# Gate and up products of the last feature pairs as seven block products, and shorter column steps

## The chip, the cores and the metric

The kernel runs on one core of a Trainium2 chip. The metric is the device time of one execution in microseconds (us): the median of the runs. The core has a matrix engine (TensorE, PE in the profile; its weight loads are PEld), VectorE (DVE), ScalarE (ACT), GpSimd (POOL) and SyncE (SP). Each runs its own instruction stream in the order in which the program emitted it, and they are kept together by semaphores. SP's and POOL's queues issue the transfers here.

## The reference

Two branches work on 2048 tokens of 576 channels and are mixed by a gate that depends on the token:

```
g = sigmoid((A_x * gate_w).sum(-1))
a = irfft2(rfft2(A_x) * (w_r + 1j * w_i))           # over tokens and channels
b = (gelu_tanh(B_x @ w_gate) * (B_x @ w_up)) @ w_down   # 576 -> 4608 -> 576
out = g * a + (1 - g) * b
```

Branch a is called the spectral branch here, branch b the dense branch. The kernel uses one input, x, for both.

## The kernel before

**The dense branch** keeps PE busy. Tokens are split in two halves `p` of 1024, each in two blocks `tb` of 512; the 4608 hidden features in 36 tiles of 128, taken two at a time, so there are 18 feature pairs for each half and 36 in all. A number is split in two parts of reduced precision, hi and lo, and a product is hi·hi + lo·hi + hi·lo. The 576 channels are four tiles of 128 and a tail of 64; the tail stands twice in one tile, so that two matmuls do its three products. So gate, or up, of one feature tile for one token block is a `chain` (L642) of 4 x 3 + 2 = 14 matmuls of 128x512 into one PSUM bank (`pgu`, two buffers). `hidden` (L675) runs the gate chain, GELU on ACT out of PSUM, the up chain, the multiplication on DVE (L688), a copy that rounds to hi on ACT (L204 is the helper of all such copies) and the low part on DVE (L693). `down` (L718) multiplies a hidden block of two features and 128 tokens with the down weights: 2 x 6 matmuls of 128x288 (L704) into `pdn`, an ACT copy that scales by 1 - g into a staging buffer (L728), and a transfer on POOL's queue that adds it to the result in DRAM (L716). Weights are loaded into `raw` (L615, L616), and split by an ACT copy and a DVE subtraction (L623).

The main loop (L842) runs over slots, one for each pair and token block: 4 chains, and 4 `down`s of the slot before. At the end (`down_end`, L761, and `down_last`, L747) the sums are read back from DRAM, added on DVE (L754) and stored to the output. Between the halves the token operands are reloaded (`reload_x`, L833; L607).

**The spectral branch** is a Python generator, `spectral` (L528): FFTs along channels on DVE for two halves of the tokens (`forward_rows`), FFTs over 16 tiles (`dft16_tiles`), 16 column blocks (`columns`, L221) with two small matrix products each on PE (`product`, L258, into `pf`, one buffer), and the way back (`inverse_rows`, L478, for each half). Its instructions are put among those of the dense branch:

- After 1 to 9 matmuls the dense branch calls `gap()` (L564): twice in each chain (L652), once in each `down` (L730), so 12 times a slot. `gap` first runs what is due at that count (`later`, filled by `at(n, fn)`: n gaps from now), then one entry of `aux`, then the generator.
- The generator is stepped while `credit[0]` is positive. `tick` (L556) adds `RATE` times the PE time of the matmuls; each step and each DVE instruction of the dense branch takes off its own cost. `yield None` ends the gap.
- `lower` (L620) makes a weight tile's low part due three gaps on; `due` (L629) runs it at once if a matmul needs it sooner.

A column step in `columns` is `STEP` = 9 gaps long (L303): the first product (g = 0), the filter on DVE (L291, L292, L299 to L301, L337, L338), the second product (g = 5) on the previous block, rounding copies and lows (L256) ahead of each, and `corner` (L243), which moves two 64-partition pieces of a tile over SP's queue, out to `cns` and back in a later gap.

Of the kernel before, what the change touches and what calls it, by code (L numbers as in the profile page):

```python
# [24 lines left out]
KT = 5  # L25
# [3 lines left out]
UNIT = ROWS // 4  # L29
RATE = 0.9  # L30
STEP = 9
ROW_BLOCK = (0, 6, 3, 5, 8, 1, 2, 7, 4)
# [125 lines left out]
def _build(nc, tc, a):  # L158
    with ExitStack() as ctx:
# [17 lines left out]
        dn = [mk(f"dn{i}", [2, D], F32R) for i in range(4)]  # L177
        raw = [mk(f"raw{i}", [KT * 256 + D]) for i in range(2)]
        hb = [mk(f"hb{i}", [2, TB], F32R) for i in range(3)]
# [41 lines left out]
        def columns():  # L221
# [62 lines left out]
            for kb in range(18):  # L284
# [18 lines left out]
                for g in range(STEP):  # L303
                    if g == 0:
                        if on:
                            v = product(0, kb, xh, xl)
                            load_ww(kb + 1)
                            corner(kb + 2, 0, False)
                        if was:
                            copy(yh, vs)  # L310
                    elif g == 1 and on:
                        copy(zr, v[:, 1, :NK])
                        vec.tensor_tensor(two(w1), two(w1), sgn[:, None, :].to_broadcast([P, 2, NK]), ALU.mult)
                    elif g == 2:
                        if was:
                            low(yl, vs, yh)
                        if kb + 1 < 16:
                            copy(xh2, two(Z[kb + 1]))
                    elif g == 3:
                        if on:  # L320
                            filter_start()
                        corner(kb - 2, 2, True)
                    elif g == 4:
                        if on:
                            corner(kb + 2, 0, True)
                        if kb + 1 < 16:
                            low(xl2, two(Z[kb + 1]), xh2)
                    elif g == 5:
                        if was:
                            w = product(1, kb - 1, yh, yl)  # L330
                        if on:
                            swap()
                    elif g == 7:
# [5 lines left out]
                    elif g == 8:  # L339
# [4 lines left out]
                    if kb == 17 and g > 5:  # L344
                        break
                    credit[0] -= 0.6 if on else 0.0
                    yield None
# [130 lines left out]
        def inverse_rows(h):  # L478
# [6 lines left out]
            yield from stage(rows, 32, range(4), 1)  # L485
            yield from small_twiddles(rows, LEFT, 1)
            yield from stage(rows, 8, range(4), 1)
            r1, r2, r3, r4, z0, i1, i2, i3, i4 = (rows[:, 512 * i:512 * (i + 1)] for i in range(9))
# [18 lines left out]
            R = rows.rearrange("p (k t) -> p t k", t=8)  # L507
            yield None
            for t in range(8):
# [108 lines left out]
        todo = {}  # L618

        def lower(key, g, r, cost):  # L620

            def run():
                vec.tensor_tensor(g[:, 1], r, f(g[:, 0]), ALU.subtract)  # L623
                credit[0] -= cost

            todo[key] = run
            at(3, lambda: due(key))

        def due(key):  # L629
            todo.pop(key, lambda: None)()  # L630

# [65 lines left out]
        def down_mm(ps, prev, t, part):  # L697
            c = slice(t * P, (t + 1) * P)
            j, h = prev[3][part]
            due(("dn", j))  # L700
# [17 lines left out]
        def down(prev, t):  # L718

            p, i, tb, _ = prev  # L720
            u = 8 * p + 4 * tb + t
# [18 lines left out]
        def rest(i):  # L740
            return st[i][:, 0:D]

# [17 lines left out]

        def down_end(prev):  # L761
            f = ps_f2()
            ps = [pair(), pair(), (f[:, 0, 0:HD], f[:, 1, 0:HD]), (ps_gu()[:, 0:HD], ps_gu()[:, 0:HD])]
            for t in range(4):
                down_last(prev, t, ps[t], 0)
            for t in range(4):
                down_last(prev, t, ps[t], 1)

# [71 lines left out]
        lows = []  # L840
        nslot = 2 * NBLK * 2
        for n in range(nslot + 1):  # L842
            p, r = divmod(n, 2 * NBLK)
            i, tb = divmod(r, 2)
            j = 2 * (p * NBLK + i)
            last = n == nslot
            if n == 2 * NBLK - 2:
                for q in range(4):
                    load_x(q)
            if n == nslot - 2:  # L850
                while gens:
                    credit[0] = 1.0
                    gap()
                for u in range(8):
                    nc.sync.dma_start(a["y"][u], yd[u])
                load_last(0)
            if n == nslot - 1:
                load_last(1)
            if n in (2 * NBLK - 1, 2 * NBLK):
                reload_x(1 - tb)  # L860
            if last:
                lows.pop()()
                down_end(prev)
                break
            ends = n == nslot - 1
            def early():
                if lows:
                    lows.pop()()

            h0, low0 = hidden(j, tb, early)  # L870
            if ends:
                for t in range(2):
                    v = pair()
                    for part in range(2):
                        down_last(prev, t, v, part)
            elif prev is not None:
                down(prev, 0)
                down(prev, 1)
            low0()
            jn = j + 2 + tb  # L880
            more = jn < 2 * NT and n > 0
            if n == 1:
                prep_gu(2)
                prep_dn(2)
            if more:
                prep_gu(jn)
            hprev = prev

            def mid():
                if ends:  # L890
                    for t in range(2, 4):
                        v = pair()
                        for part in range(2):
                            down_last(hprev, t, v, part)
                elif hprev is not None:
                    down(hprev, 2)
# [3 lines left out]
            if more:  # L900
                prep_dn(jn)
                for q in ((4, 5) if n == 1 else (jn + 2,)):
                    if q < 2 * NT:
                        at(3, lambda q=q: load_w(q))
            lows.append(low1)
            prev = (p, i, tb, ((j, h0), (j + 1, h1)))

# [49 lines left out]
```

## Time and profile before

| | |
|---|---|
| median of 3 runs | 1421.62 us (1421.54 to 1423.27) |
| profiled execution | 1421.89 us, span from first to last instruction 1420.1 us |
| busy: PE, DVE, ACT, POOL | 1409.4, 885.8, 641.2, 264.3 us |
| column stage (first to last product) | 458.9 to 726.5 us |
| last small twiddle of the way back, second half (L126) | 1058.9 us |
| last store of the spectral branch (L521) | issued at 1135.1 us |
| granted TensorE clock, mean | 0.998 |

A row that groups instructions gives: line, engine, operation, output <- input, shapes, count | busy us, mean ns | idle us of the engine before them, and what ended it. A row of the order of time gives: start us, duration us, engine, line, operation, and in brackets an idle time before it with its releaser. A row of waits gives: engine, tile and line that waited, what it waited for, total us, times, longest. A row of windows gives: stretch, length, then busy us and (count) of PE, PEld, DVE, ACT and POOL, the granted clock, the DMA engines' busy share and GB/s. A row of one line's instructions gives: engine, operation, output <- input, count: least, median and largest ns, first and last start in us. A row of transfers gives: target <- source, queue, count, KB each, median us from issue to landing. PE's durations are modelled and overlap; its pitch is read from the starts.

### The profile page before, as it was taken

How to read it: one execution, taken by the hardware profiler on the slowest of the kernel's cores; microseconds unless marked ns; L12 is line 12 of the kernel's file. 1: busy time of each engine (PE TensorE's matmuls, PEld its weight loads, DVE VectorE, ACT ScalarE, POOL GpSimd, SP SyncE). 2: the span in 40 equal slices, each digit the busy share in tenths (PEclk: the TensorE clock that was granted, in tenths of full speed). 3: DMA queues.
4: the chain of work that ended last, by engine and by line, in shares of the span. 5: the costliest groups of instructions: out<-in, count | busy, mean ns of one | idle time of the engine just before them, and what ended most of it. 6: DMA issues, size and time to landing. Idle time of an engine off the chain costs nothing.

```text
span 1420.1 us, 19578 instructions
## 1 busy us (share of the span) xinstructions
PE 1409.4 (99%) x7686; PEld 1245.2 (88%) x7686; DVE 885.8 (62%) x1160; ACT 641.2 (45%) x956; POOL 264.3 (19%) x321
## 2 busy tenths in 40 slices
PE   9999999999999999999999999999999999999998
PEld 7888888888888889888888888888888888888887
DVE  5978758797785656655658878774878522222223
ACT  5534454444454555555645453436343533333331
POOL 0011121111112122222110211114111321111110
PEclk9999999999999999999999999999999999999999
DMA  7466666556668789899863556569656776665754
GB/s 258 147 121 118 116 163 120 105 111 120 120 112 202 178 200 197 207 227 197 212 141 121 109 100 111 112 121 186 114 96 115 143 144 120 121 112 110 163 96 123
DMA packets 90813, 201.94 MB, mean 142 GB/s; under 512 B 11104, under 2 KB 21344, under 8 KB 90336
## 3 DMA queue, kind: packets, MB, share of 16 engines
q0 software_dynamic: 44928, 90.98, 43.0%
q1 hardware_dynamic: 45792, 109.70, 24.7%
q8 instruction: 60, 0.98, 0.3%
q14 instruction: 33, 0.27, 0.1%
HBM read 101.48 MB, written 92.01 MB: 136 GB/s over the span
## 4 chain that ended last, share of the span: by engine, by line
PE 98%; DMA 1%; ACT 0%; SPq 0%; DVE 0%; issue 0%; DVEq 0%
PE pdn L704 32%; PE pgu L647 18%; PE pgu L649 18%; PE pgu L648 18%; PE pgu L654 5%; PE pgu L653 5%; PE pf L263 2%; DMA til<-xt 1%; DVE til L754 0%; ACT stg L728 0%; ACT gu L204 0%; SPq L779 0%; SPq L778 0%; PE pf L704 0%; PE pgu L704 0%
## 5 line engine op out<-in xcount | busy, mean ns | idle before, releaser
L704 PEld LDWEIGHTS pdn<-dn,hb 128*128 128x128 f32 x3432 | 471.6, 188 | 11.3 <-ACT til L204 0.2
L704 PE MATMUL pdn<-dn,hb 128*128 128x288 f32 x3432 | 479.3, 295 | 0.0
L647 PE MATMUL pgu<-xhi,gu 128*128 128x512 f32 x1144 | 447.7, 391 | 1.3 <-ACT gl L682 1.3
L649 PE MATMUL pgu<-xlo,gu 128*128 128x512 f32 x1144 | 446.5, 390 | 0.0
L648 PE MATMUL pgu<-xhi,gu 128*128 128x512 f32 x1144 | 446.3, 390 | 0.0
L716 POOL DMA_DIRECT2D yd<-stg x264 | 230.3, 873 | 1070.2 <-ACT stg L728 1031.8
L688 DVE TENSOR_TENSOR gl<-gl,pgu 128x512 f32<-128x512 f32 x144 | 98.9, 687 | 336.6 <-PE pgu L654 336.3
L204 ACT ACTIVATE hb<-gl 128x512 fp32r<-128x512 f32 x144 | 91.2, 633 | 438.9 <-DVE gl L688 438.9
L728 ACT ACTIVATE stg<-pdn,omg 128x576 f32<-128x576 f32 x272 | 201.7, 742 | 168.1 <-PE pdn L704 165.8
L649 PEld LDWEIGHTS pgu<-xlo,gu 128*128 128x128 f32 x1144 | 215.0, 188 | 46.6
L647 PEld LDWEIGHTS pgu<-xhi,gu 128*128 128x128 f32 x1144 | 215.1, 188 | 40.9 <-ACT gl L682 1.7
L648 PEld LDWEIGHTS pgu<-xhi,gu 128*128 128x128 f32 x1144 | 215.0, 188 | 39.0
L623 DVE TENSOR_TENSOR gu<-raw,gu 128x1280 fp32r<-128x1280 f32 x70 | 104.3, 1489 | 79.0 <-ACT gu L204 78.7
L685 ACT ACTIVATE gl<-pgu 128x512 f32<-128x512 f32 x143 | 85.5, 598 | 144.1 <-PE pgu L654 143.9
L693 DVE TENSOR_TENSOR hb<-gl,hb 128x512 fp32r<-128x512 f32 x144 | 99.0, 688 | 31.1 <-ACT hb L204 30.9
L653 PE MATMUL pgu<-xtl,gu 128*128 128x512 f32 x286 | 111.4, 389 | 0.0
L654 PE MATMUL pgu<-xtl,gu 128*128 128x512 f32 x286 | 111.4, 389 | 0.0
L204 ACT ACTIVATE gu<-raw 128x1280 fp32r<-128x1280 f32 (+2 forms) x77 | 92.2, 1197 | 4.9 <-DMA raw<-wgu 4.6
L653 PEld LDWEIGHTS pgu<-xtl,gu 128*128 128x128 f32 x286 | 53.7, 188 | 11.3
L654 PEld LDWEIGHTS pgu<-xtl,gu 128*128 128x128 f32 x286 | 53.7, 188 | 11.1
L623 DVE TENSOR_TENSOR dn<-raw,dn 128x576 fp32r<-128x576 f32 x72 | 54.1, 751 | 1.3 <-ACT dn L204 1.3
L92 DVE TENSOR_TENSOR rows<-rows 128x1280 f32<-128x1280 f32 x36 | 53.6, 1489 | 0.7
(116 smaller groups left out, 862.6 us busy)
## 6 DMA issues: line engine op xcount, KB each, us to landing
yd<-stg POOLq DMA_DIRECT2D x264, 288.0 KB, 5.1
raw<-wgu SPq DMA_DIRECT2D x70, 640.0 KB, 5.5
raw<-wd SPq DMA_DIRECT2D x72, 288.0 KB, 2.8
colm<-col POOLq DMA_DIRECT2D x32, 256.0 KB, 5.9
tmp<-wf SPq DMA_DIRECT2D x16, 290.0 KB, 5.4
cns<-til SPq DMA_DIRECT2D x64, 72.5 KB, 4.9
til<-cns SPq DMA_DIRECT2D x64, 72.5 KB, 4.3
misc<-wf SPq DMA_DIRECT2D x16, 290.0 KB, 5.5
```

Source lines behind the costliest of these rows:

```text
L204: act.activation(o, i, AF.Copy)
L623: vec.tensor_tensor(g[:, 1], r, f(g[:, 0]), ALU.subtract)
L647: pe.matmul(ps, w[:, 0, k, c], xhi[tb][:, k], start=k == 0, stop=False)
L648: pe.matmul(ps, w[:, 1, k, c], xhi[tb][:, k], start=False, stop=False)
L649: pe.matmul(ps, w[:, 0, k, c], xlo[tb][:, k], start=False, stop=False)
L653: pe.matmul(ps, w[:, 0, 4, c], xtl[tb], start=False, stop=False)
L654: pe.matmul(ps, w[:, 1, 4, c], xtl[tb], start=False, stop=True)
L688: vec.tensor_tensor(g, g, pu, ALU.mult)
L693: vec.tensor_tensor(h[:, 1], g, f(h[:, 0]), ALU.subtract)
L704: pe.matmul(ps[half], h[:, l, c], d[:, q, half * HD:(half + 1) * HD], start=part == 0 and n == 0, stop=part == 1 and n == 2)
L716: pl.dma_start(yd[u], o, accum_op=ALU.add)
L728: put(u, lambda o: act.activation(o.rearrange("p (c k) -> p c k", c=2), v[:, :, 0:HD], AF.Copy, scale=omg[:, u:u + 1]), i == 0)
```

## The change

**Block products.** For the second half of the tokens, gate and up of a pair are seen as a 2x2 block product: two token blocks by two halves of the channels (288 each), times two halves of the channels by two feature tiles. Seven block products with sums and differences of blocks (Strassen, in Winograd's form) give the same four results as eight. A half of the channels is two tiles of 128 and a tail of 32 that stands four times in one tile, so one matmul does the tail. One block product of one of gate and up is 2 x 3 + 1 = 7 matmuls (`seven`), a product has two of these. The seven products write to `pgu` and `pf` in turn; DVE adds each to running sums in SBUF; for each finished block GELU, multiplication, copy and low follow in later gaps.

The weights of the seven products (`prep_b`) are differences of blocks on DVE, then hi (ACT, 768 columns) and low (DVE, 512 columns on 128 and 256 on 64 partitions), two products ahead, in four slots of the old `gu` buffers. The token operands are built once by the generator `operands`, after the spectral branch has freed its memory, and `late_operands` adds one that needs the buffers of the ordinary chains.

**The switch.** `inverse_rows(1)` sets `free` after its small twiddles. The pair that then begins still loads weights as before, the next one loads the first blocks, and from there on pairs are done by `products`; with this schedule these are the last nine. `finale` takes the place of `down_end`. The second half's spectral result is now added through the staging buffers (`put`), one every four gaps.

**Spectral pace.** `RATE` is 0.95 instead of 0.9, a column step has 7 gaps instead of 9 and takes 6.4 instead of 5.4 of credit. The first product stays at g = 0; the filter moves from g = 3 to 2, ahead of the low that was at 2; the second product from g = 5 to 4; the corner's way back on the second side from four gaps after its way out to two, on the first side from four to three.

`lower` and the new preparations go through `seq`, which makes several steps due at several counts; `due` now runs all that are left.

The diff, cut to its core (new helpers `tail_of`, `late_operands`, `load_b`, `load_d` and the host's packing are left out; `load_b` and `load_d` issue the loads on SP's queue):

```
-RATE = 0.9
-STEP = 9
+RATE = 0.95
+STEP = 7
...
-                    elif g == 1 and on:
-                        copy(zr, v[:, 1, :NK])
-                        vec.tensor_tensor(two(w1), two(w1), sgn[:, None, :].to_broadcast([P, 2, NK]), ALU.mult)
+                    elif g == 1:
+                        if on:
+                            copy(zr, v[:, 1, :NK])
+                            vec.tensor_tensor(two(w1), two(w1), sgn[:, None, :].to_broadcast([P, 2, NK]), ALU.mult)
+                        if kb + 1 < 16:
+                            copy(xh2, two(Z[kb + 1]))
+                        corner(kb - 2, 2, True)
                     elif g == 2:
+                        if on:
+                            filter_start()
                         if was:
                             low(yl, vs, yh)
...
                     elif g == 3:
                         if on:
-                            filter_start()
-                        corner(kb - 2, 2, True)
...
-                    elif g == 5:
+                    elif g == 4:
                         if was:
                             w = product(1, kb - 1, yh, yl)
...
+        def seq(key, *steps):
+
+            q = todo[key] = [fn for _, fn in steps]
+            for n, _ in steps:
+                at(n, lambda: q and q.pop(0)())
+
+        def due(key):
+            q = todo.pop(key, [])
+            while q:
+                q.pop(0)()
...
+        def prep_b(i, m, lead=0):
...
+            def total():
+                for o, p, q in ((), (), ((r11, r12, r11), (tsum, r22, r11)), ((r12, r22, r12),), (),
+                                ((r21, r21, tsum),), ())[m]:
+                    vec.tensor_tensor(o, p, q, ALU.subtract)
+                    credit[0] -= 0.95
+
+            def high():
+                copy(w[:, 0:768], x)
+
+            def low():
+                vec.tensor_tensor(w[:, 768:1280], x[:, 0:512], f(w[:, 0:512]), ALU.subtract)
+                vec.tensor_tensor(w[64:128, 512:768], x[64:128, 512:768], f(w[64:128, 512:768]), ALU.subtract)
...
+            seq(("b", i, m), (lead, total), (lead + 2, high), (lead + 4, low))
+
+        def seven(ps, i, m, x, s):
+
+            due(("b", i, m))
...
+            for t in range(2):
+                c = slice(256 * t + P * s, 256 * t + P * (s + 1))
+                pe.matmul(ps, hi[:, c], xh[:, t], start=t == 0, stop=False)
+                pe.matmul(ps, lo[:, c], xh[:, t], start=False, stop=False)
+                pe.matmul(ps, hi[:, c], xl[:, t], start=False, stop=False)
+            pe.matmul(ps, w[:, 512 + P * s:512 + P * (s + 1)], xt, start=False, stop=True)
+            tick(7 * 0.2265)
+            gap()
+
+        def products(i, spare, pend, early):
...
+                seq((name, i), (1, lambda: act.activation(g, g, AF.Gelu_apprx_tanh)), (2, mult),
+                    (3, lambda: copy(h[:, 0], v)), (5, low))
...
+            for n, (name, nd) in enumerate((("a11", 2), ("a12", 2), ("s2", 1), ("s3", 1), ("s1", 1), ("a22", 1),
+                                            ("s4", 0))):
+                m = n + 2
+                prep_b(i + m // 7, m % 7, 2 if m in (7, 9) else 0)
...
+                if n % 2:
+                    y = ps_f2()
+                    ps = [y[:, s] for s in range(2)]
+                else:
+                    ps = [ps_gu() for _ in range(2)]
+                for s in range(2):
+                    seven(ps[s], i, n, name, s)
+                    due({1: ("c12", i - 1), 3: ("c21", i - 1), 4: ("c11", i), 6: ("c22", i)}.get(n))
+                    if n == 0:
+                        copy(u[s], ps[s])
+                    for o, x in (((), ((c, u),), ((u, u),), ((u3, u),), ((c, u3), (u, u)), ((u3, u3),), ((c, u),))[n]):
+                        add(o[s], x[s], ps[s])
+                    if n == 0 and s == 0:
+                        early()
+                k = {1: ("c11", c), 4: ("c22", c), 5: ("c21", u3), 6: ("c12", c)}.get(n)
+                if k:
+                    finish(*k)
+                for _ in range(nd):
+                    if pend:
+                        d, t = pend.pop(0)
+                        down(d, t)
...
+            if state or p == 1 and tb == 0 and free[0]:
+                state += tb == 0
+            if state == 3:
+                break
...
+        late_operands()
...
+        for i in range(i, NBLK):
...
+            products(i, spare, pend, early)
+        finale(pend)
```

In `finale` the four `down`s of the second token block run one after another, then those of the first block in four PSUM places, all first parts ahead of all second parts.

More of the change, by code (lines that the diff above doesn't have):

```diff
@@ L508, in inverse_rows @@
             yield None
+            if h == 1:
+                yield from operands()
+                for t in range(8):
+                    u = 8 + t
+                    put(u, lambda o: act.activation(o, R[:, t, 0:D], AF.Copy, scale=gs[:, u:u + 1]), False)
+                    for _ in range(4):
+                        yield None
+                return
             for t in range(8):
@@ L759, in pair, with tail_of @@
             return v[:, 0, 0:HD], v[:, 1, 0:HD]
[L761 to L767, printed above, removed]
+        ops = {}
+        free = [False]
+        def tail_of(o, x):
+            copy(o, x)
+            for q in (32, 96):
+                r = slice(q, q + 32)
+                vec.tensor_tensor(o[r], x[r], f(o[r]), ALU.subtract)
```

224 lines of the change are left out of this document (170 added, 54 removed).

## The prediction

> **What bounds the kernel now.** I read the page first (busy time, slices, chain), then the waits of the matrix engine, then windows and the order of time where something was odd.
>
> ```profile
> span 1420.1 us, 19578 instructions
> PE 1409.4 (99%) x7686; PEld 1245.2 (88%) x7686; DVE 885.8 (62%) x1160; ACT 641.2 (45%) x956; POOL 264.3 (19%) x321
> DVE  5978758797785656655658878774878522222223
> PE 98%; DMA 1%; ACT 0%; SPq 0%; DVE 0%; issue 0%; DVEq 0%
> PE pf L263 <- ACT gu L204: 2.9, 1, 2.9
> PE pgu L647 <- ACT gl L682: 1.3, 1, 1.3
> ```
>
> PE is the chain (98%), and its only wait after the start is one of 2.9 us. Only fewer matmuls or a shorter matmul can make this kernel faster; whatever delays PE by a microsecond makes it that much slower. VectorE (DVE) has room in the last seven slices, where the spectral branch has ended, and little before.
>
> The price of a matmul comes from the order of time, since the listed durations overlap:
>
> ```profile
> 1199.10 0.39 PE L647 MATMUL pgu<-xhi,gu 128*128 128x512 f32 x1
> ...
> 1202.27 0.39 PE L647 MATMUL pgu<-xhi,gu 128*128 128x512 f32 x1
> ...
> 1205.45 3.35 PE L704 MATMUL pdn<-dn,hb 128*128 128x288 f32 x24
> 1205.72 0.69 DVE L688 TENSOR_TENSOR gl<-gl,pgu 128x512 f32<-128x512 f32 x1 [3.60 <-PE pgu L654]
> 1206.44 0.63 ACT L204 ACTIVATE hb<-gl 128x512 fp32r<-128x512 f32 x1 [3.31 <-DVE gl L688]
> 1207.10 0.69 DVE L693 TENSOR_TENSOR hb<-gl,hb 128x512 fp32r<-128x512 f32 x1 [0.70 <-ACT hb L204]
> ...
> 1208.63 0.40 PE L647 MATMUL pgu<-xhi,gu 128*128 128x512 f32 x1
> ```
>
> From 1199.10 to 1205.45 are two chains of 14: 3.18 us a chain, 0.227 us a matmul. 24 down matmuls take 1208.63 - 1205.45 = 3.18 us, so one `down` takes 1.59 us. A pair of features has 8 chains and 8 downs: 38.2 us. DVE begins 0.27 us after the next PE work would begin (1205.72 against 1205.45).
>
> **The block products.** A pair's 8 chains (112 matmuls) become 7 products of 14 (98): one chain, 3.18 us, saved a pair, and 9 x 3.18 = **28.6 us** for nine pairs. Shapes are the same (128x512 moving), so the pitch is kept. The downs stay 8 a pair.
>
> For that, DVE and ACT work more. The nearest rows:
>
> ```profile
> L688 DVE TENSOR_TENSOR gl<-gl,pgu 128x512 f32<-128x512 f32 x144 | 98.9, 687 | 336.6 <-PE pgu L654 336.3
> L623 DVE TENSOR_TENSOR gu<-raw,gu 128x1280 fp32r<-128x1280 f32 x70 | 104.3, 1489 | 79.0 <-ACT gu L204 78.7
> L800 DVE TENSOR_TENSOR gu<-raw,gu 128x256 fp32r<-128x256 f32 x5 | 2.1, 423 | 3.8 <-ACT gu L204 3.8
> ```
>
> Per pair DVE does 14 additions out of PSUM (0.687 each, 9.6 us), 4 weight differences of 768 columns (between 0.687 and 1.489, by length 0.955: 3.8), 7 weight lows of 512 and of 256 columns (0.69 + 0.423: 7.8), 2 down lows of 576 (by length 0.755: 1.5), and for 4 hidden blocks a product and a low (0.687 + 0.69 each: 5.5): 28.2 us, against 10.0 before (2 x 1.489 + 1.5 + 5.5). A pair will take 35 to 37 us, so DVE is about 77% busy. That is what it is in the window 40 to 456 quoted below, where PE never waits. ACT gets some 19 us a pair. So the engines have the capacity, and the cost lies in the **order** of DVE's queue. I went through one pair with these durations, product by product (14 matmuls, then its downs; 2, 2, 1, 1, 1, 1, 0 of them). A product's sums must be out of PSUM before the second next product uses the same banks. They are: the fifth product's four additions end 1.5 us after it, and the seventh begins 6.4 us after it (two downs and a product). Seven being odd, the next pair's first product takes the seventh's banks at once, but half by half, and the first half's addition is out 0.6 us before (1.59 - 0.27 - 0.69). The weights are ready too, with one exception.
>
> That is the border between two pairs. The weights of the next pair's first product are prepared with a lead of 2, so their low is due at 6 gaps, and only 5 gaps come (two half products and one down, then two half products and no down). It is therefore forced by `due` when that product begins, and it stands in DVE's queue behind the last additions of the seventh product, which wait for PE. From the end of that product: 0.27 until DVE starts, 0.69 addition, 0.69 low, and 0.15 back to PE (the row pair 4.55 + 0.42 to 5.12, below) make 1.8 us; PE has one matmul to do meanwhile (0.23). **1.6 us at each of 8 borders, 12.8 us.** Bounds: 0, if the low comes earlier than I read; 2.9 (the only wait of PE this trace has) each.
>
> ```profile
> 4.55 0.42 DVE L803 CAST xhi<-til 128x512 fp32r<-128x512 f32 x1
> ...
> 5.12 2.04 PE L666 MATMUL pgu<-xhi,gu 128*128 128x512 f32 x4 [0.74 <-DVE xhi L803]
> ...
> 15.14 0.50 PE L647 MATMUL pgu<-xhi,gu 128*128 128x512 f32 x1 [1.33 <-ACT gl L682]
> ```
>
> The **opening** of the first block pair: after the last ordinary chain DVE's queue holds the hidden product (0.27 to 0.96), then the late operands, each low behind an ACT copy (0.63): 0.69 twice, then two tails of 0.69, until 5.0; then the second weight differences, 2 x 0.955; only then the low of the last hidden block, at 7.6. PE does two half products (3.18), one part of a down (0.8) and four matmuls (0.53), and needs that low at 4.5: **3.3 us** of waiting. At the **end**, the first down follows the seventh product at once and needs the low of its first block: 0.27 + 0.69 + 0.69 + 0.15 - 0.53 = 1.3; and a PSUM pair is used again 0.45 us too soon: **1.8 us** in all. The results of the other half are read back some 5 us before they are needed (a store lands in 5.1 us, the load in 3.2), and are hidden.
>
> ```profile
> yd<-stg POOLq DMA_DIRECT2D x264, 288.0 KB, 5.1
> raw<-wgu SPq DMA_DIRECT2D x70, 640.0 KB, 5.5
> ...
> til<-yd SPq DMA_DIRECT2D x8, 288.0 KB, 3.2
> ```
>
> The loads: 4 x 384 + 2 x 288 KB a pair against 2 x 640 + 2 x 288, and 12 of 256 KB for the token blocks, all on SP's queue; 256 KB more in 36 us. Weight block 22 is the tightest: issued after its low in the sixth product, about 6.7 us before the pair's end, 384 KB land in 3.2 to 5.5 us (rows of 288 and 640 KB), and DVE wants it 2 us after the border. Hidden by 3 us.
>
> **The clock.** The one PE wait in the middle of the trace shows that a wait costs more than itself:
>
> ```profile
> 706.06 0.40 PE L649 MATMUL pgu<-xlo,gu 128*128 128x512 f32 x1
> 709.34 1.79 PE L263 MATMUL pf<-colm 128*128 128x290 f32 x6 [2.88 <-ACT gu L204]
> ...
> 712.63 0.40 PE L648 MATMUL pgu<-xhi,gu 128*128 128x512 f32 x1
> ```
>
> ```profile
> 710.00:711.00 1.00, 1.00 (x6) 1.00 (x6) 1.00 (x1) 0.71 (x2) 0.00 (x0) 0.50 1.06 258
> ```
>
> PE should have gone on at 706.29 and did at 709.34: 3.05 us lost. Then the granted clock was 0.50 until about 712.6, and 6 product matmuls (0.133 each, like the down matmuls) and 4 wide ones took 3.29 us in place of 1.71: another 1.58. The event cost 4.6 us. The opening wait of 3.3 us is longer than this one, so I add **1.6 us** for its clock. The borders' 1.6 us are shorter; the wait of 1.33 us at 15.14 was followed by a clock of 1.00:
>
> ```profile
> 15.00:20.00 5.00, 4.86 (x21) 4.05 (x22) 3.02 (x6) 3.12 (x7) 0.00 (x0) 1.00 1.00 412
> ```
>
> The Trainium skill ("TensorE: Matmul & The Clock Gate", Part 1) states that the clock halves after an idle window of about 3.4 us. By that figure the opening wait would cost no clock and the sum would be 1.6 us lower. The trace shows the drop after 3.05 us, and I go by the trace.
>
> **The spectral branch sooner.**
>
> ```profile
> 40.00:456.00 416.00, 416.00 (x2262) 366.97 (x2262) 322.14 (x407) 188.92 (x284) 74.13 (x88) 1.00 0.63 126
> 456.00:730.00 274.00, 271.12 (x1517) 241.59 (x1516) 159.91 (x246) 148.92 (x230) 59.18 (x78) 0.99 0.87 199
> L126 DVE SCALAR_TENSOR_TENSOR rows<-rows,tmp x32: 314/318/327, 107.4 to 1058.9; 128x160 f32<-128x160 f32 x32
> L607 DVE TENSOR_TENSOR xlo<-xraw,xhi x8: 682/684/694, 697.9 to 727.1; 128x512 fp32r<-128x512 f32 x8
> cns<-til SPq DMA_DIRECT2D x64, 72.5 KB, 4.9
> ```
>
> The matmuls of this branch are the same, so by itself it saves PE nothing. 18 column steps shrink by 2 gaps of 1.59 us (57 us in all), and the rate of 0.95 lets some 6% more through where credit is the limit; the last small twiddles, which set the switch, move from 1059 to some 960. A pair starts at about 42 + 38.2 n, so the switch falls in pair 24, the two pairs of transition are 25 and 26, and nine remain, as the change says. A pair more or less would move the time by 3.2 - 1.6 = 1.6 us only.
>
> The rows show what it does besides. The column stage ran from 456 to 730 and overlapped the reload of tokens (697.9 to 727.1), which is tied to PE's progress; in that overlap the 4.6 us event fell, DVE and ACT having queued the reload's copies ahead of the filter that PE waited for. After the change the columns end near 660, and the event goes: **-4.6 us** (bounds 0 and -4.6). The reload then meets long butterfly operations in a denser queue: **+1.0** (bounds 0 and 4.6, another such event). In the tighter column step the second product comes two gaps after its low instead of three, and the low stands behind the two filter additions. Two gaps are 2.05 us at the least (three and six wide matmuls); filter and low take 0.46 + 0.46 + 0.76 = 1.7. Most steps pass; bounds 0 and 16 x 0.76 = 12.2; I take **+1.5**, near the lower end, since today's 16 steps pass with no wait outside the reload. The corner's second transfer is issued 2 gaps (3.2 us) after a first that lands in 4.9, so SP stands still 1.7 us a step; behind it wait the weight loads, which land in 5.5 us and are used some 16 us after issue. Hidden. The spectral stretch at the end becomes operand work and 8 more stores through the staging buffers, in gaps where PE does not depend on them.
>
> **Sum**, against the profiled execution's 1421.9: -28.6 - 4.6 + 12.8 + 3.3 + 1.6 + 1.8 + 1.5 + 1.0 = -11.2, 1410.7. The median of the runs is 0.3 lower: **1410.4 us**. Its own range is 1404 to 1416.
>
> **Rivals.**
> (a) *No border wait.* The forced low is ready in time after all. For it: nothing in the rows, only that the queue order was read from code. 1410.4 - 12.8 = 1397.6.
> (b) *The column step waits.* Each of 16 steps loses the 0.76 of the low that now stands behind the filter: 1410.4 + 12.2 - 1.5 = 1421.1, no change. For it: DVE and ACT are in order and the event at 709 was of this kind; against: 14 other steps without a wait.
> (c) *The borders lose the clock.* 8 x 1.58 more: 1423.0, no change. Against: the 1.3 us wait at the start.
> (d) *DVE becomes the bound of a block pair*, slower. Its 28.2 us are tied to PE's sums on one side and ACT's copies on the other (idle 0.70 before a low, above); if the handover of each of the other six products waits for just one addition, PE loses 54 x 0.69 = 37 us: 1447. It decides from (11.2 + 2.8) / 54 = 0.26 us a product. Against: 8 us of free DVE time in a pair.
> (e) *The switch comes late* and fewer pairs are changed: eight give 1412, within the forecast.
>
> **Chances.** About 0.2% (2.8 us) is what a measurement of this kernel can tell from no change. Forecast with (e) 0.62, (a) 0.16, (b) 0.07, (c) 0.05, (d) 0.10. Faster: 0.62 + 0.16 and a little of (b), 0.80; same 0.10; slower 0.10. The range goes from (a) with its own spread to just short of (b): 1396 to 1419.
>
> **What would show it.** Right: about 126 fewer 512-column matmuls; in the last 320 us a PE wait of 1.3 to 1.9 us on DVE at each border of a pair (some 36.4 us apart), one of about 3 us with a clock below 1 in the first block pair; no wait near 709; DVE 7 or 8 tenths busy to the end. Wrong: border waits missing (a); waits of PE on the column products between 430 and 660 (b); a clock below 1 at each border (c); PE waiting for additions inside the pairs (d).

## The result, and the profile after

| | before | after |
|---|---|---|
| median of the runs | 1421.72 us | 1458.68 us (1457.53 to 1460.13) |
| ratio to before | | 1.0258 [1.024, 1.0276] |
| profiled execution, its span | 1421.89, 1420.1 us | 1458.89, 1457.1 us |
| PE instructions | 7686 | 7560 |

The change made the kernel 37 us slower; the forecast was 11 us faster. The page of the changed kernel (span; busy time; DVE in 40 slices; the chain that ended last, by engine):

```profile
span 1457.1 us, 19840 instructions
PE 1398.1 (96%) x7560; PEld 1219.6 (84%) x7560; DVE 1056.9 (73%) x1460; ACT 685.0 (47%) x1038; POOL 263.5 (18%) x321
DVE  6989668886866666757889883988567666666665
PE 82%; DVE 9%; issue 4%; ACT 2%; DMA 2%; SPq 0%; DVEq 0%; ACTq 0%
```

The 126 matmuls are gone as forecast, but PE, 99% busy before, is at 96%, and DVE holds 9% of the chain. DVE itself is 6 to 7 tenths busy in the last slices, less than forecast. An engine that is less busy than planned and still delays PE points to order, not capacity. The waits of PE (who, on whom: us in total, times, longest) name it:

```profile
PE pf L902 <- DVE xraw L931: 30.2, 27, 1.9
PE pgu L903 <- DVE gu L886: 9.6, 9, 1.1
PE pgu L662 <- DVE gl L703: 5.8, 3, 2.8
PE pdn L720 <- DVE hb L708: 3.5, 3, 3.0
```

The first row is not in the forecast's sum: 27 waits are three in each of nine pairs. The second is the border: eight of its nine waits lie between two pairs, one at the opening. Here is one pair in the order of time, the three waits on `pf` first, each with the addition that it waits for (L931), then the border:

```profile
1201.60 0.40 PE L905 MATMUL pf<-sx,gu 128*128 128x512 f32 x1
1202.04 0.69 DVE L931 TENSOR_TENSOR xraw<-gl,pf 128x512 f32<-128x512 f32 x1 [0.76 <-PE pf L905]
1202.78 0.50 PE L902 MATMUL pf<-xhi,gu 128*128 128x512 f32 x1 [0.78 <-DVE xraw L931]
...
1214.53 0.42 DVE L887 TENSOR_TENSOR gu<-raws,gu 64x256 fp32r<-64x256 f32 x1
1214.98 0.69 DVE L931 TENSOR_TENSOR xraw<-gl,pf 128x512 f32<-128x512 f32 x1
...
1215.73 0.50 PE L902 MATMUL pf<-sx,gu 128*128 128x512 f32 x1 [1.45 <-DVE xraw L931]
...
1225.43 0.69 DVE L920 TENSOR_TENSOR xraw<-xraw 128x512 f32<-128x512 f32 x1 [0.58 <-ACT xraw L927]
1226.04 0.68 DVE L931 TENSOR_TENSOR xraw<-xraw,pf 128x512 f32<-128x512 f32 x1
...
1226.78 0.50 PE L902 MATMUL pf<-xhi,gu 128*128 128x512 f32 x1 [1.11 <-DVE xraw L931]
...
1233.33 0.40 PE L902 MATMUL pgu<-xhi,gu 128*128 128x512 f32 x1
1233.53 0.69 DVE L931 TENSOR_TENSOR xraw<-gl,pgu 128x512 f32<-128x512 f32 x1 [0.61 <-PE pgu L905]
1234.13 0.68 DVE L886 TENSOR_TENSOR gu<-raws,gu 128x512 fp32r<-128x512 f32 x1
1234.87 0.50 PE L903 MATMUL pgu<-xhi,gu 128*128 128x512 f32 x1 [1.15 <-DVE gu L886]
```

At 1201.60 PE issues the last matmul of a product's first half (gate). It should begin the second half (up) at 1201.83. It begins at 1202.78, when DVE's addition of the *first* half has ended. DVE was idle for 0.76 us before that addition, so its queue was not the cause here: it began 0.21 us after the second half could have. PE waits for a reader of a result that it is not about to overwrite. In the code both halves are slices of one tile (`y = ps_f2()`, `ps = [y[:, s] for s in range(2)]`), while the products on `pgu` use two separate tiles and show no such wait. With the first matmul after a wait (0.34 us to the next start, against 0.23) the three places cost 1.06 + 1.73 + 1.37 = 4.16 us a pair, 37.4 us in nine. At the second and third place DVE had no idle time before the addition (1214.98 and 1226.04 follow other work): there its queue was late too, and made the wait 0.67 and 0.31 us longer than at the first. That is 0.98 us a pair, some 8.8 of the 37.4.

The border is as the forecast drew it: the last addition, then the forced low, then PE, 1.41 us later than it could (1233.56 to 1234.87, and 0.1 for the next start). The pair, from the first matmul of its second product to the same of the next pair, is the window from 1200.22 below: 40.96 us, of which PE is busy for 36.47. It was 38.2 before and was forecast at 34.97 + 1.6.

Ahead of the block pairs and at their opening, the same view (a third wait on `gl`, of 0.84 us, stands at 392.80):

```profile
219.70 0.50 PE L662 MATMUL pgu<-xhi,gu 128*128 128x512 f32 x1 [2.81 <-DVE gl L703]
...
727.09 0.79 PE L662 MATMUL pgu<-xhi,gu 128*128 128x512 f32 x1 [2.18 <-DVE gl L703]
...
1078.36 3.65 PE L720 MATMUL pdn<-dn,hb 128*128 128x288 f32 x14 [3.05 <-DVE hb L708]
```

And the windows (stretch; length; PE, PEld, DVE, ACT, POOL busy and count; granted clock; DMA share; GB/s), the first from before, the others from after:

```profile
0.00:1065.36 1065.36, 1058.96 (x5767) 935.08 (x5768) 762.89 (x995) 512.42 (x778) 197.81 (x245) 1.00 0.69 148
```

```profile
0.00:1069.90 1069.90, 1060.33 (x5766) 934.81 (x5767) 805.23 (x1060) 516.29 (x789) 197.61 (x246) 1.00 0.70 149
438.00:649.00 211.00, 211.00 (x1197) 188.67 (x1196) 138.32 (x216) 124.15 (x192) 49.69 (x68) 1.00 0.92 213
1200.22:1241.18 40.96, 36.47 (x196) 30.74 (x195) 26.69 (x43) 17.91 (x27) 6.90 (x9) 1.00 0.59 111
220.00:221.00 1.00, 1.00 (x6) 0.79 (x5) 0.94 (x2) 1.00 (x3) 0.00 (x0) 1.00 0.55 179
```

The first two rows hold the same work (PE's counts differ by one): the block pairs begin 4.5 us later than the same point of before. The columns' stretch, 438 to 649, has no wait at all (PE 211.00 of 211.00).

### The profile page after: what moved, and what is told of

It is laid out like the page before. It is cut to its first block, busy times and chain, and to the rows that moved or that the text cites. A ratio compares the mean times of both kernels' runs of the same rounds, so it can differ in the third digit from the quotient of the medians.

```text
span 1457.1 us, 19840 instructions
## 1 busy us (share of the span) xinstructions
PE 1398.1 (96%) x7560; PEld 1219.6 (84%) x7560; DVE 1056.9 (73%) x1460; ACT 685.0 (47%) x1038; POOL 263.5 (18%) x321
## 4 chain that ended last, share of the span: by engine, by line
PE 82%; DVE 9%; issue 4%; ACT 2%; DMA 2%; SPq 0%; DVEq 0%; ACTq 0%
PE pdn L720 27%; PE pgu L662 12%; PE pgu L664 12%; PE pgu L663 12%; PE pgu L669 3%; PE pgu L668 3%; PE pgu L903 2%; PE pgu L904 2%; PE pgu L902 2%; PE pf L264 2%; PE pf L902 2%; DVE xraw L931 1%; PE pf L904 1%; PE pf L903 1%; PE pgu L905 1%
## 5 line engine op out<-in xcount | busy, mean ns | idle before, releaser
L720 PEld LDWEIGHTS pdn<-dn,hb 128*128 128x128 f32 x3000 | 415.2, 189 | 16.3 <-DVE hb L708 4.2
L720 PE MATMUL pdn<-dn,hb 128*128 128x288 f32 x3000 | 424.1, 296 | 3.7 <-DVE hb L708 3.5
L662 PE MATMUL pgu<-xhi,gu 128*128 128x512 f32 x856 | 335.7, 392 | 6.9 <-DVE gl L703 5.8
L664 PE MATMUL pgu<-xlo,gu 128*128 128x512 f32 x856 | 334.3, 390 | 0.0
L663 PE MATMUL pgu<-xhi,gu 128*128 128x512 f32 x856 | 334.2, 390 | 0.0
L662 PEld LDWEIGHTS pgu<-xhi,gu 128*128 128x128 f32 x856 | 161.1, 188 | 37.8 <-DVE gl L703 7.4
L663 PEld LDWEIGHTS pgu<-xhi,gu 128*128 128x128 f32 x856 | 161.1, 188 | 28.9
L205 ACT ACTIVATE gu<-raws 128x1280 fp32r<-128x1280 f32 (+3 forms) x104 | 106.9, 1029 | 5.9 <-DMA raws<-wgu 5.3
L642 DVE TENSOR_TENSOR gu<-raws,gu 128x1280 fp32r<-128x1280 f32 x52 | 77.3, 1487 | 28.2 <-ACT gu L205 28.1
L669 PE MATMUL pgu<-xtl,gu 128*128 128x512 f32 x214 | 83.3, 389 | 0.0
L668 PE MATMUL pgu<-xtl,gu 128*128 128x512 f32 x214 | 83.3, 389 | 0.0
L720 PEld LDWEIGHTS pdn<-dn,gu 128*128 128x128 f32 x432 | 59.0, 188 | 3.8 <-DVE gu L924 2.3
L720 PE MATMUL pdn<-dn,gu 128*128 128x288 f32 x432 | 60.4, 295 | 1.9 <-DVE gu L924 1.9
L931 DVE TENSOR_TENSOR xraw<-gl,pf 128x512 f32<-128x512 f32 x36 | 24.7, 687 | 43.7 <-PE pf L905 43.4
```

The lines of the kernel that those rows point to most:

```text
L205: act.activation(o, i, AF.Copy)
L662: pe.matmul(ps, w[:, 0, k, c], xhi[tb][:, k], start=k == 0, stop=False)
L663: pe.matmul(ps, w[:, 1, k, c], xhi[tb][:, k], start=False, stop=False)
L664: pe.matmul(ps, w[:, 0, k, c], xlo[tb][:, k], start=False, stop=False)
L668: pe.matmul(ps, w[:, 0, 4, c], xtl[tb], start=False, stop=False)
L669: pe.matmul(ps, w[:, 1, 4, c], xtl[tb], start=False, stop=True)
```

## The experiments

The theory after the result: the tile of `pf` orders its halves, about 37 us; the borders cost 11; the denser spectral pace costs some 5. The main rival is the forecast's own (d), DVE as the bound of a block pair.

**The two halves of `pf` as two tiles, the rest as changed.** In the columns, the copy that read both halves becomes two copies.

```
-            return psum.tile([P, 2, 512], F32, name="pf2", tag="pf2", bufs=1)
+            return [psum.tile([P, 512], F32, name="pf2", tag="pf2", bufs=2) for _ in range(2)]
...
-                            copy(two(Z[kb - 1]), w[:, :, :NK])
+                            for al in range(2):
+                                copy(two(Z[kb - 1])[:, al], w[al][:, :NK])
...
-                    y = ps_f2()
-                    ps = [y[:, s] for s in range(2)]
+                    ps = ps_f2()
```

> The changed kernel with pf as two PSUM tiles of one bank each, in place of one tile of two banks; the column stage reads them with two ACT copies instead of one. Theory 1 (one tile): in the products that write to pf, PE's second half waits for DVE's addition out of the first half, only because both halves are one tile; the 27 waits of PE on L931 (1.38 us each with the slower matmul behind them) go, -37 us: about 1421.5 us. Rival (DVE late): DVE is behind with its additions whatever the tiles are; the waits stay or move to another line, above 1450 us.

Measured: 1422.2 us, ratio to before 1.000 [0.9988, 1.0011]. The first row of PE's waits, and the same place of a product on `pf` in the order of time:

```profile
PE pgu L904 <- DVE gu L887: 9.9, 9, 1.2
```

```profile
1153.20 0.40 PE L906 MATMUL pf<-sx,gu 128*128 128x512 f32 x1
...
1153.44 0.39 PE L903 MATMUL pf<-xhi,gu 128*128 128x512 f32 x1
...
1153.64 0.69 DVE L932 TENSOR_TENSOR xraw<-gl,pf 128x512 f32<-128x512 f32 x1 [0.71 <-PE pf L906]
```

All 27 waits on `pf` are gone, and the time falls by 36.5 us with DVE's work unchanged. The second half begins 0.24 us after the last matmul of the first, and DVE reads the first half while PE writes the second: the hardware didn't need the order that the single tile imposed. The Trainium skill ("PSUM — Partial Sum Buffer", PSUM bank collisions raise a hardware error) says that two engines on different banks run clean, and asks to guard PSUM by bank; each half is one bank of 512 numbers, and this run agrees.

**The border's preparation as early as the others.**

```
-                prep_b(i + m // 7, m % 7, 2 if m in (7, 9) else 0)
+                prep_b(i + m // 7, m % 7)
```

> The changed kernel with the lead of 0 for the first weights of the next pair too, so that their low is due before the seventh product's additions. Theory (queue order): the 8 border waits of PE on the weights' low (1.15 us idle, 1.41 with the slow matmul behind them) go, -11 us: about 1447.5 us. Rival (load late): the low waits for its load or its ACT copy instead and the border stays: within 3 us of 1458.7.

Measured: 1448.22 us, 1.0184 [1.0167, 1.0202]. In PE's list of waits the row of the border (L903 on `gu`) is no longer there, and the first row is the one of the changed kernel to the digit (L902 on L931: 30.2, 27, 1.9). So the lead of 2 cost 10.5 us (1458.68 - 1448.22), and has nothing to do with the waits on `pf`. It bought little: without it, the longest wait for the low of a hidden block (L720 on L924), behind the first border, is 1.8 us in place of 1.0.

**Both.** The diff is that of the two above.

> Both edits. If the two kinds of waits are separate, the gains add up: 1458.7 - 37 - 11 = about 1410.5 us, which is the blind forecast. Rival (DVE late): with the false waits gone DVE, 28 us of work in a 35 us pair, becomes the next wait and at least a third of the 48 us stays: above 1425 us.

Measured: 1414.78 us, 0.9953 [0.9937, 0.997], faster than before by 7. The start of one pair and of the next in the order of time, and a window inside it:

```profile
1151.19 0.39 PE L903 MATMUL pf<-xhi,gu 128*128 128x512 f32 x1
...
1186.63 0.39 PE L903 MATMUL pf<-xhi,gu 128*128 128x512 f32 x1
```

```profile
1155.00:1190.00 35.00, 35.00 (x192) 30.69 (x192) 26.23 (x42) 17.81 (x27) 6.91 (x8) 1.00 0.67 129
```

PE is busy for all of the 35 us, while DVE is 75% busy (26.23 of 35), as forecast (77%). That settles rival (d): DVE's load does not bind a pair. The pair lasts 35.44 us, 0.47 more than 98 matmuls at 0.227 and 8 downs at 1.59 (34.97). The two savings, 36.5 and 10.5, should have made 1411.7; 3.1 us of that didn't come. One part is seen: the wait for a low behind the first border is 1.80 us, as with the border's edit alone, against 1.00 with the tiles split alone. The rest was not followed, and it is no more than what executions of one kernel differ by: the ten with the tiles split range from 1418.50 to 1425.81 us.

**The spectral pace alone, on the kernel before.**

```
-RATE = 0.9
-STEP = 9
+RATE = 0.95
+STEP = 7
...
-                    credit[0] -= 0.6 if on else 0.0
+                    credit[0] -= 6.4 / STEP if on else 0.0
```

and the new order of the column step.

> The kernel before with the new spectral pace alone (RATE 0.95, STEP 7 and the reordered column step), no block products. From the changed trace, whose first block pair starts 4.6 us later than that pair did before: about 1426 us, from waits of PE on the hidden product behind DVE's longer queue. The blind forecast's own terms for it (-4.6 + 1.5 + 1.0) would give 1419.6 us.

Measured: 1426.8 us, 1.0038 [1.0023, 1.0053]. PE's largest group of waits is on `gl` (6.0 us, 4 times). The first large one in the order of time, and the window behind it:

```profile
219.47 0.80 PE L646 MATMUL pgu<-xhi,gu 128*128 128x512 f32 x1 [2.82 <-DVE gl L687]
```

```profile
220.00:221.00 1.00, 1.00 (x4) 0.74 (x3) 0.93 (x3) 1.00 (x3) 0.00 (x0) 0.50 0.39 128
```

Without block products the pace by itself costs 4.9 us, where the forecast's terms for it made -2.1. What PE waits for is no column product but the multiplication of the dense branch (`gl`), which stands in DVE's queue behind more spectral work than before.

**Where the rest could be had.** Four runs on top of "both"; the kernel before, measured beside them, took 1423.12 us. First, the tiles behind `msk` moved to multiples of 64 bytes, for the 0.47 us a pair:

```
-        msk = mk("msk", [2 + 96])
+        msk = mk("msk", [112])[:, 0:98]
```

> e3_both with the mask tile made 112 columns wide instead of 98, so that every tile behind it (the sums of token blocks, in sx, among them) starts 32 bytes later, at a multiple of 64 bytes. In the traces a wide matmul follows the one before by 0.2335 us in products that read sx, against 0.227 in chains, whose operands start at multiples of 64. Theory (alignment): the pitch in those products falls to 0.227, 5 of 7 products, 9 pairs x 70 x 0.0065 = -4 us: 1410.7. Rival (it is the weights or the order): the pitch and the time stay, 1414.8.

Measured: 1413.12 us, 0.994 [0.9925, 0.9955]. A product that reads `sx`, and the down behind it:

```profile
1157.67 0.40 PE L903 MATMUL pgu<-sx,gu 128*128 128x512 f32 x1
...
1160.93 0.30 PE L721 MATMUL pdn<-dn,hb 128*128 128x288 f32 x1
```

14 matmuls still take 3.26 us, 0.233 each. The products that take only their tail from `sx` did become faster: the last product of one pair and the first of the next, 28 matmuls up to the first `down`, take 6.39 us (1177.06 to 1183.45) in place of 6.48 in "both" (1176.95 to 1183.43). From that `down` to the same one of the next pair:

```profile
1183.45 3.34 PE L721 MATMUL pdn<-dn,gu 128*128 128x288 f32 x24
...
1218.81 3.35 PE L721 MATMUL pdn<-dn,gu 128*128 128x288 f32 x24
```

A pair is 35.36 us, against 35.44 (1183.43 to 1218.87) without this edit: the shift took 0.08 of the 0.47 us. Alignment to 64 bytes is not the main cause.

Second, the old rate until slot 38 of the main loop, then 0.97:

```
-            credit[0] += RATE * us
+            credit[0] += rate[0] * us
...
+            if n == 38:
+                rate[0] = 0.97
```

with `rate = [0.9]` at the start; eight pairs are block pairs then.

> e3_both with the rate of the spectral branch at 0.9 in the first 38 slots, as before the change, and at 0.97 after that; the switch then falls one pair later, so eight pairs are block products. Theory (queue length): the PE waits on the hidden product at 220, 393 and 727 us (2.80, 0.84 and 2.17 us, and 1.5 for the clock) come from the rate of 0.95 and go; the lost pair costs 3.18 - 0.3: 1414.8 - 7.3 + 2.9 = 1410.4. Rival (the shorter column step is to blame): the waits stay and only the pair is lost, 1417.7.

Measured: 1412.0 us, 0.9926 [0.9914, 0.9938]. The waits at 220 and 393 are gone, but one of 3.15 us came at 742. By then 1728 down matmuls are done, those of 36 slots; each slot runs the downs of the one before, so PE is in slot 37, and the rate is still the old one. Third, the preparations that `early` holds put ahead of the late operands at the opening:

```
+        early()
         late_operands()
```

> e3_both with the last ordinary hidden block's low emitted ahead of the late operands instead of behind them and the second weight differences. Theory (queue order): PE's wait of 3.05 us at 1079 and its slow clock (1.6) go, 1410.1. Rival: what was pushed back (late operands, first weights) is waited for in its place; half or more stays, above 1412.5.

Measured: 1410.45 us, 0.9909 [0.9895, 0.9923]. At the opening, in the order of time:

```profile
1080.13 0.50 PE L904 MATMUL pf<-xhi,gu 128*128 128x512 f32 x1 [1.04 <-DVE gu L887]
```

The 3.05 us wait became one of 1.04, and the granted clock behind it stayed at 1.00. So the opening was a matter of order, as forecast, and most of it could be had back. Fourth, all of these together, eight pairs again:

> All three edits on e3_both. If each holds and they are separate: 1414.8 - 4 - 4.4 - 4.6 = 1401.8. Without the alignment 1405.8; with the opening alone 1410.

Measured: 1408.92 us, 0.9903 [0.9891, 0.9916], against 1405.8 expected without a gain from alignment. Its interval and that of the opening alone (0.9909) overlap, so they are not told apart; both beat the kernel before by about 0.9%, and the change by 3.3 to 3.4%. A wait of 3.14 us at 744 is still there.

**What the wait near 740 hangs on.** The rate at 0.9 until slot 41, past that place, then 0.95; on top of "both" and the opening:

```
+            if n == 41:
+                rate[0] = 0.95
```

> e3_both with the opening's order mended as in e7_open and the rate at 0.9 in the first 41 slots, 0.95 after; eight pairs are block products. Theory (queue length): neither the waits at 220 and 393 us (rate 0.95) nor the one of 3.15 us at 742 (rate 0.97 from slot 38) come, so some 3 to 4.5 us under the 1408.9 of e8_all: about 1405. Rival (the rate is not the cause): a wait of the same kind falls elsewhere before 1060 us, 1408 to 1411.

Measured: 1415.18 us, 0.9944 [0.993, 0.9958], a miss. Order of time, DVE and PE:

```profile
737.96 2.56 DVE L92 TENSOR_TENSOR rows<-til 128x2320 f32<-128x2320 f32 x1
740.56 2.58 DVE L92 TENSOR_TENSOR til<-til 128x2320 f32<-128x2320 f32 x1
...
743.79 0.50 PE L664 MATMUL pgu<-xhi,gu 128*128 128x512 f32 x1 [3.13 <-DVE gl L705]
...
745.30 0.63 PE L664 MATMUL pgu<-xhi,gu 128*128 128x512 f32 x1
...
1090.42 0.69 DVE L818 TENSOR_TENSOR misc<-xraw 128x512 f32<-128x512 f32 x1 [9.40 <-DMA xraw<-xs]
...
1095.42 0.79 PE L664 MATMUL pgu<-xhi,gu 128*128 128x512 f32 x1 [5.82 <-DVE gl L705]
```

And a pair of such operations in the kernel before, where PE doesn't wait:

```profile
740.81 0.69 DVE L688 TENSOR_TENSOR gl<-gl,pgu 128x512 f32<-128x512 f32 x1 [5.67 <-PE pgu L654]
741.42 2.57 DVE L92 TENSOR_TENSOR rows<-til 128x2320 f32<-128x2320 f32 x1
```

At the old rate the wait of 3.13 us is there all the same: two long operations of the spectral branch on DVE (2.56 and 2.58 us) stand ahead of the multiplication (L705) that PE needs. The rate is therefore the cause of the waits at 220 and 393, which are gone here as in the other runs at 0.9, and not of this one; the expectation blamed the rate of 0.97 for it, which had not begun by then. In the kernel before, the multiplication (L688) stands just ahead of such operations and not behind them. So the wait hangs on where they fall in DVE's queue. That the shorter column step put them there is not shown: the step alone was not run. A new wait of 5.82 us fell into the last slots ahead of the switch: DVE stood still for 9.40 us until a load of token blocks had come, and then did 4.3 us of work on the new operands (1090.42 to 1094.68) before it came to the multiplication. The two waits, 9.0 us together, are of the size of the miss (10 us).

**The 0.47 us a pair.** Two kernels, on top of "both" and the opening. In one, the products that should read sums of token blocks read the operand `a22`, which stands outside `sx`; in the other the values of `a22` are copied to where the sums stand. The tails in `sx` are treated likewise. Both leave the sums out of the products, so only the pitch is compared.

```
+            one = ops["a22"]
+            for n in ("s1", "s2", "s3"):
+                ops[n] = one
...
```

> e7_open in which the products that should read the sums of token blocks (s1, s2, s3) and the tails in sx read the fourth token block (a22, outside sx) instead; instructions, shapes and waits are the same, the sums of tokens are left out of the products. Theory (operand): a product's 14 wide matmuls then take 3.2 us in place of 3.26, 0.227 to 0.230 us each, and a pair is 0.3 to 0.5 us shorter. Rival (weights or order of the matmuls): the pitch stays 0.2335 in the third and fourth product.

```
+            one = ops["a22"]
+            for n in ("s1", "s2", "s3"):
+                for o, x in zip(ops[n], one):
+                    copy(o, f(x))
...
```

> e7_open with the fourth token block's values copied over the sums in sx once, ahead of the products (the sums are left out of the products; six more ACT copies at the opening, a few us). The place read is that of the change, the values those of e10_operand. If the slower pitch comes from the place, it stays 0.2335 in the third and fourth product; if it comes from the values, it is that of e10_operand.

Measured: 1411.27 and 1421.26 us, one profiled execution each; the second has additional copies at the opening, so times of the pair are compared, not of the kernel. The first `down` pair of one block pair and of the next in the order of time, with `a22` itself and then with its copy:

```profile
1183.37 3.35 PE L721 MATMUL pdn<-dn,gu 128*128 128x288 f32 x24
...
1218.42 3.35 PE L721 MATMUL pdn<-dn,gu 128*128 128x288 f32 x24
```

```profile
1191.12 3.36 PE L721 MATMUL pdn<-dn,gu 128*128 128x288 f32 x24
...
1226.56 3.36 PE L721 MATMUL pdn<-dn,gu 128*128 128x288 f32 x24
```

35.05 and 35.44 us; without these edits a pair takes 35.44 (1151.19 to 1186.63, above). The same values read from the place of `sx` cost the full 0.39 us a pair, read from the place of `a22` they don't. It is where the moving operand stands, not what it holds. Which property of the place it is stays open: the 64-byte alignment of `sx`, tried above, is worth 0.08 us of it. The other 0.08 of the 0.47 us (35.05 against 34.97) is there with `a22` too.

## Why the prediction was wrong

Set against the measured 37.0 us (1458.89 - 1421.89), the forecast's sum stands like this:

| term | forecast | measured |
|---|---|---|
| 126 matmuls fewer | -28.6 | -28.6 |
| spectral pace: event at 709, column step, reload | -2.1 | +4.5 |
| opening, its clock included | +4.9 | +6.6 |
| eight borders | +12.8 | +11.3 |
| inside the pairs | 0 | +37.4 |
| pitch of the matmuls | 0 | +4.2 |
| end | +1.8 | +1.4 |
| sum | -11.2 | +36.8 |

**The step that failed** is "A product's sums must be out of PSUM before the second next product uses the same banks. They are". The capacity and the distance between products were right; the step had no price in the sum, and the runs showed 37.4 us in its place. What I missed is that the two halves of one product on `pf` share a tile, so that the second half of *the same* product waits for the reading of the first. I had even used the right picture at the border, where the `pgu` halves are taken "half by half", and applied it to `pf` without asking whether its halves were separate buffers. The profile of before could not show it, since nothing there reads one half of `pf` while the other is still to be written. The code quoted in the diff did: one `ps_f2()`, two slices. With two tiles the 36.5 us came back.

**Rival (d)** gave 1447 and was nearest, but by another mechanism. Its 37 us were 54 handovers of 0.69 behind a loaded DVE; the trace has 27, at 1.06 to 1.73 us each. Its sign, PE waiting for additions inside the pairs, did come, and DVE's queue lengthened two waits in three, by 8.8 us in all; but PE needed none of these additions. That the sums agree is chance: the run with both edits has the same DVE load, and inside the pair shown there PE doesn't wait.

**The pace** was mis-sized. The event at 709 went, and the columns have no wait between 438 and 649, which refutes rival (b). But the forecast looked for the price inside the column step and at the reload only. The reload's term of +1.0 (bounds 0 and 4.6) measured 3.9: 2.34 us late at 727.09, and 1.6 for the clock behind it. The waits at 219.70 and 392.80, some 3.1 and 1.1 us late, lie in the stage on rows, where I had taken the rate of 0.95 as free because PE never waited there at 0.9. DVE was 77% busy there already (322.14 of 416.00 us, a row that the forecast quotes); that this left no room for more was not read from it. The three make 8.1, and 8.1 - 4.6 = 3.5 of the measured 4.5 (1069.90 against 1065.36); 1.0 is not placed.

**The pitch** "is kept, shapes are the same" was off by 0.47 us a pair: the operands stand elsewhere.

**What was right:** the count of matmuls; the border, its mechanism and its size (1.6 forecast, 1.41 measured), without a loss of clock, so that rivals (a) and (c) fall; the opening's 3.3 us (3.22 late, from 1075.14 to 1078.36) with a slower clock behind it (14 down matmuls took 3.45 us from there, against 1.86 at 0.133 each: 1.6). That the clock fell there was in part luck: behind the same wait of 3.05 us, the kernel with the two tiles did the 14 matmuls in 1.95 us (1079.83 to 1081.78). Waits of 0.40 and 1.00 us for two other lows, one at the first product and one behind the first border, came on top. The end measured 1.4 of 1.8.

Had the one step been right, the rest of the sum would have given about 1421, no change: the borders and the pace ate the gain that the 126 matmuls brought. The versions with order mended are 12 to 14 us faster than the kernel before, of the 28.6.

## What to carry to other kernels

Slices of one buffer were one dependence here: where one engine is to read the first part while another writes the second, make them separate buffers (here one PSUM bank each), which costs nothing in space and was worth 36 us. When a change gives a second engine more to do, go through its queue for each hand-over, and look at the busy share stage by stage only to see whether it can fit at all. Work that is "only moved earlier" off the critical path still stands in a queue, and its long operations can fall on someone else's need there.

## What the runs showed of the hardware

The length of a wait alone doesn't decide whether the clock is lost. A wait of 2.82 us at 219.47 (the pace alone) was followed by a clock of 0.50, and matmuls 0.43 us apart; nearly the same wait at 219.70 in the changed kernel, 2.81 us, was not: the window 220 to 221 of after, above, has a clock of 1.00. The wait of 2.18 us at 727.09 lost it (8 matmuls took 3.42 us from there, 0.43 each). And behind the wait of 3.13 us at 743.79 the clock held for six matmuls and fell only at 745.3, 1.5 us after PE had gone on (0.63 us a matmul from there).

The extremes are further apart. Three rows, from the run with the opening's order mended, from "both", and from the run that reads `a22`:

```profile
1110.44 4.45 PE L721 MATMUL pdn<-dn,gu 128*128 128x288 f32 x20 [1.82 <-DVE gu L925]
```

```profile
1112.99 2.92 PE L721 MATMUL pdn<-dn,gu 128*128 128x288 f32 x20 [1.80 <-DVE gu L925]
```

```profile
1076.77 0.47 PE L911 MATMUL pgu<-xtl,gu 128*128 128x512 f32 x1 [3.50 <-DVE xtl L797]
```

The first two are the same wait of 1.8 us at the same place. In one execution the 20 matmuls behind it took 4.29 us to the next start, with a clock of 0.63 from 1111 to 1112; in the other they took 2.76 us. The wait of 3.50 us in the third was followed by a clock of 1.00 (1077 to 1081).

The Trainium skill ("TensorE: Matmul & The Clock Gate", Part 1) describes a free-running window of about 3.4 us in which activity is judged. That the outcome depends on where in such a window a wait falls would fit these rows, though none shows the window itself; that about 3.4 us of idleness are needed does not, since 1.8 us were enough. After the first 15 us of the traces, waits up to 1.5 us were never seen to cost clock here.
